# Order of the setup loads and of the second modulation in an adaLN block with windowed attention and a bilinear MLP

## The chip, the cores and the metric

The kernel runs on one core of one Trainium2 chip. The metric is the device time of one execution in microseconds (us). Three runs of the kernel before gave 594.92, 594.03 and 593.01 us, median 594.03. One further execution was recorded by the hardware profiler; its span, from the first to the last instruction, is 594.0 us, and every position below is given in us from the start of that span.

## The reference

The input `x` has 2048 rows of 576 numbers. One conditioning row `c` gives six vectors of 576, by `silu(c) @ w_mod`, with `w_mod` of 576 x 3456:

```
sa, ca, ga, sb, cb, gb = split(silu(c) @ w_mod, 6)
h = layernorm(x) * (1 + ca) + sa          # first modulation
x = x + ga * attention(h, wqkv, wo)       # each row looks at itself and 7 rows before, 2 apart; 32 heads of 18
h = layernorm(x) * (1 + cb) + sb          # second modulation
x = x + gb * ((h @ w_gate) * (h @ w_up)) @ w_down      # 4608 hidden columns
```

Matrices are bf16. Nearly all of the arithmetic is in the last line.

## The kernel before, in words

The rows are cut into ten chunks, four of 128 rows and six of 256 (`SIZES`, L34). Each chunk goes through `project` (LN, modulation, q, k and v; L424) and `attend` (logits, softmax, weighted sum, output projection `wo`, second LN and modulation into `h2T`; L499). Both are Python generators: each `yield` is a place where the caller can go on with something else, so the order in which the caller advances them is the order of the instructions. `gate_up` (L608) then runs the 4608 hidden columns for a pass of one or two chunks, in nine blocks of 512 columns, and `down` (L664) multiplies by `w_down`. While one pass of `gate_up` runs, a `Pacer` slips in the attention of the next chunk.

**The setup** is L737 to L777 and is the only part that the change touches. There the order on every computing engine is the order of the program (`manual_schedule` over all of them). It works off chunk 0 up to its `h2T` and chunk 1 up to its q, k and v, and in between makes the modulation vectors:

- `mod_columns` (L229) multiplies two of the six vectors' weights with the silu row by 40 small matmuls, so that they lie along partitions; `mod_pick` (L249) takes the right elements out by a multiplication with a diagonal and a sum on VectorE. It is called for `sa, ca` (buffer `wmA`) and for `sb, cb` (buffer `wmB`).
- `mod_row_mm` and `mod_row_copy` (L257, L264) make `ga` and `gb` as rows that are equal on all partitions, by ten matmuls each (L261) and two copies on ScalarE (L265, L266). Their weights are the two halves of `wmC`.
- `warm(n)` (L268) issues `n` matmuls on zeros, whose result nobody reads.

The three weight buffers come from a pool of two, so `wmB` takes the place of `wmA` once that has been used.

**Loads.** SyncE's queue (q1) brings `wqk`, `wv`, rows of `x` and the gate weights. GpSimd's queue (q0) brings, in the order of the program: both row loads of `load_first` (each made of a main part over 128 partitions and a rest over 64), `wo` in four loads of 32 partitions each (L200), the up weights of the hidden blocks (`load_up`, L205), the `gb` half of `wmC` (`load_gb`, L202), the stores of v to a DRAM scratch `vd` (L487), and the reloads of v shifted by the window into `vsh` (L497). A program order on GpSimd means that an issue which must wait holds back all later ones. Up weights of blocks 0 and 1 go to buffers of their own (`gm`), those of blocks 2 to 5 to places inside the buffer that `w_down` takes later (`wd`).

**Chunk 0's attention** has a form of its own: `attn` is shifted by eight small matmuls (`up`, L557), VectorE copies it (L558) and multiplies it with v (four L563), and 40 matmuls with shifted identities add the eight products up, transposed, into `oTs` (L573). Two copies (L587, L588), ten matmuls with `wo` (`pw`, L594), the gate by `ga` (L599), the residual (L600), then LN2 (L369 to L385), transposes (L406) and the second modulation (L416, L418) end in `h2T`.

The middle of the setup before:

```python
        go(b0, "up")        # chunk 0's logits and softmax
        next(a0, None)      # chunk 0's v
        next(a1)            # chunk 1's v
        load_up([1, 2, 3])
        mod_row_mm(wmC, 0)
        mod_row_copy(0, ga_bc)
        next(b0)            # up matmuls, first product
        pmB = mod_columns(wmB, 0)
        go(b0, "oT")
        mod_pick(pmB, 2)
        next(a1)            # chunk 1's first q
```

Of the kernel before, what the change touches and what calls it, by code (L numbers as in the profile page):

```python
# [18 lines left out]
D = 576  # L19
DP = 640  # L20
KT = 5
H = 32
DH = 18
# [36 lines left out]
def kernel(  # L60
# [13 lines left out]
    nc = tc.nc  # L74
# [40 lines left out]
    for sl, m0, off in ((slice(0, KT), 0, 0), (slice(KT, KT + 1), KT - 1, -64)):  # L115
        n = sl.stop - sl.start
# [9 lines left out]
    wo = wts.tile([P, KT, D], BF, name="wo")  # L126
# [23 lines left out]
    def load_rows(eng, dst, src):  # L150

        eng.dma_start(dst[:, 0:KT - 1, :], src[0:(KT - 1) * P, :].rearrange("(k p) n -> p k n", p=P))
        eng.dma_start(dst[0:64, KT - 1, :], src[(KT - 1) * P:D, :])
# [25 lines left out]
    def wm_tile():  # L179
        return sp.tile([P, KT, 2 * D], BF, name="wm", bufs=2)  # L180

    nc.sync.dma_start(c_row[:], c[0, :].rearrange("(m p) -> m p", p=64))
    wmA, wmC = wm_tile(), wm_tile()
# [8 lines left out]
    wmB = wm_tile()  # L192

    def load_first():

        load_rows(nc.gpsimd, wmC[:, :, 0:D], w_mod[:, 2 * D:3 * D])
        load_rows(nc.gpsimd, wmB, w_mod[:, 3 * D:5 * D])
        for dl in range(4):
            nk = len(range(dl, DH, 4))
            nc.gpsimd.dma_start(wo[dl * H:(dl + 1) * H, 0:nk, :], A_wo.rearrange("(h d) n -> h d n", d=DH)[:, dl::4, :])  # L200

    def load_gb():  # L202
        load_rows(nc.gpsimd, wmC[:, :, D:2 * D], w_mod[:, 5 * D:6 * D])

    def load_up(blocks):  # L205

        for b in blocks:
            load_gm(gu_blocks[b][0], b, 1, nc.gpsimd)

    def kp(kt):  # L210
        return slice(0, P) if kt < KT - 1 else slice(0, 64)

    def silu_c():

        pc = att([P, 10], BF, "pc")
        for o in range(2):
            nc.tensor.transpose(pc[64 * o:64 * (o + 1), 0:9], c_row[:], identw[0:9, HALO:HALO + 9])
        nc.vector.tensor_copy(c_f[0:64, :], pc[0:64, :].rearrange("p (k o) -> p k o", o=2)[:, :, 0])
        nc.vector.tensor_copy(c_f[64:, 0:KT - 1], pc[64:, 0:8].rearrange("p (k o) -> p k o", o=2)[:, :, 1])
        e_f = sp.tile([P, KT], F32, name="e_f")  # L220
        nc.scalar.activation(e_f[:], c_f[:], ACTF.Exp, scale=-1.0)
        nc.vector.tensor_scalar_add(e_f[:], e_f[:], 1.0)
        nc.vector.reciprocal(e_f[:], e_f[:])
        nc.vector.tensor_tensor(sc32[:], c_f[:, :, None].to_broadcast([P, KT, H]), e_f[:, :, None].to_broadcast([P, KT, H]), ALU.mult)
        nc.gpsimd.tensor_copy(sc_bc[:], sc32[:, :, 0:1].to_broadcast([P, KT, P]))

        nc.vector.tensor_reduce(diag[:], ident.rearrange("p (b j) -> p j b", j=32), axis=AX.X, op=ALU.add)

    def mod_columns(wm, fill):  # L229

        pm = ps_mlp.tile([P, 2, 512], F32, name="pm", tag="mlp")
        pv = pm[:, 0, 0:2 * KT * 32].rearrange("p (v m j) -> p v m j", v=2, j=32)
        for kt in range(KT):
            if fill and kt % 2 == 0:
                warm(fill)
            w = wm[kp(kt), kt, :].rearrange("p (v f) -> p v f", v=2)
            wmain = w[:, :, 0:512].rearrange("p v (m g j) -> p v m g j", g=4, j=32)  # L240
            for last in range(2):
                for g in range(4):
                    gs = slice(32 * g, 32 * g + 32)
                    rhs = w[:, :, 512 + 32 * (g % 2):544 + 32 * (g % 2)] if last else wmain[:, :, :, g, :]
                    nc.tensor.matmul(pv[gs, :, KT - 1, :] if last else pv[gs, :, 0:KT - 1, :], lhsT=sc32[kp(kt), kt, :], rhs=rhs,
                                     start=(kt == 0 and not last), stop=(kt == KT - 1), skip_group_check=True)
        return pv

    def mod_pick(pv, vi):  # L249
        pick = sp.tile([P, 2, KT, 32], F32, name="pick", bufs=1)  # L250
        nc.vector.tensor_tensor(pick[:], pv, diag[:, None, None, :].to_broadcast([P, 2, KT, 32]), ALU.mult)
        nc.vector.tensor_reduce(modc[:, vi:vi + 2, :], pick[:], axis=AX.X, op=ALU.add)
        nc.vector.tensor_scalar_add(modc[:, vi + 1, :], modc[:, vi + 1, :], 1.0)

# [2 lines left out]
    def mod_row_mm(wm, gi):  # L257
        pr = rows[gi] = ps_mlp.tile([P, 2, 512], F32, name="pr", tag="mlp")
        for b, c0, c1 in ((0, 0, 512), (1, 512, D)):
            for kt in range(KT):  # L260
                nc.tensor.matmul(pr[:, b, 0:c1 - c0], lhsT=sc_bc[kp(kt), kt, :], rhs=wm[kp(kt), kt, gi * D + c0:gi * D + c1],  # L261
                                 start=(kt == 0), stop=(kt == KT - 1))

    def mod_row_copy(gi, dst):  # L264
        nc.scalar.copy(dst[:, 0:512], rows[gi][:, 0, :])  # L265
        nc.scalar.copy(dst[:, 512:D], rows[gi][:, 1, 0:64])  # L266

    def warm(n):  # L268

        pw = ps_mlp.tile([P, 2, 512], F32, name="warm", tag="mlp")  # L270
        for _ in range(n):
            nc.tensor.matmul(pw[:, 0, :], lhsT=zeros[:, 0:P], rhs=zeros[:, 0:512], start=True, stop=True)
# [7 lines left out]
    def load_gm(gm, b, t, eng):  # L280
        eng.dma_start(gm[:, :, t, :], (B_w_gate, B_w_up)[t][0:(KT - 1) * P, b * FB * P:(b + 1) * FB * P].rearrange("(k p) n -> p k n", p=P))
# [73 lines left out]
    def setup_late():  # L355
        setup_guard.__exit__(None, None, None)
        late_once = pool("late", 1)
        late["hh"] = late_once.tile([P, FT, CM], BF, name="hh")
        late["gup"] = pool("gup", 2)
# [331 lines left out]
    def attend_into_place(ci):  # L691
        di, c0 = home[ci]
        if di not in h2T:
            h2T[di] = h2p.tile([P, KT, CM], BF, name="h2T")
        return attend(ci, h2T[di][:, :, c0:c0 + SIZES[ci]])
# [36 lines left out]
    def go(g, label):  # L732
        while next(g, None) != label:
            pass


    with tc.manual_schedule(engines=COMPUTE):  # L737
        a0, a1, b0 = project(0), project(1), attend_into_place(0)
        warm(5)
        silu_c()  # L740
        next(a0)
        warm(4)
        pmA = mod_columns(wmA, 1)
        mod_pick(pmA, 0)
        next(a0)
        warm(9)
        next(a0)
        load_first()
        load_up([0])
        load_gb()  # L750
        next(a1)
        go(a0, "qkr")
        next(a1)
        next(a0)
        go(a1, "v0")
        go(b0, "up")
        next(a0, None)
        next(a1)
        load_up([1, 2, 3])
        mod_row_mm(wmC, 0)  # L760
        mod_row_copy(0, ga_bc)
        next(b0)
        pmB = mod_columns(wmB, 0)
        go(b0, "oT")
        mod_pick(pmB, 2)
        next(a1)
        next(b0)
        go(b0, "ln2")
        go(a1, "qkr")
        next(b0)  # L770
        mod_row_mm(wmC, 1)
        warm(5)
        go(b0, None)
        go(a1, None)
        mod_row_copy(1, gb_bc)
        load_up([4, 5])
        setup_late()  # L777

    passes = [(di, p) for di, d in enumerate(DOWN) for p in d]
# [49 lines left out]
```

## Time and profile before

| what | value |
|---|---|
| device time, median of 3 (lowest to highest) | 594.03 us (593.01 to 594.92) |
| span of the profiled execution | 594.0 us |
| TensorE matmul busy | 574.0 us (97%), 5286 matmuls |
| VectorE, ScalarE, GpSimd busy | 316.3, 270.9, 61.6 us |
| bytes moved by DMA | 76.47 MB, of them q0 28.14 MB and q1 44.29 MB |
| first matmul of `gate_up` | at 43.21 us |
| mean granted TensorE clock | 0.994 of full speed |

The page gives shares over the whole span, and TensorE is busy nearly all of it. The setup is the first 43 us of that, and must be read by itself: from the answers that list the instructions in order of time, from the chain of waits cut to this stretch, and from the loads with their time from issue to landing. A row of the instruction list has the start, the busy time, the engine, the line and the tiles, and in brackets how long the engine stood idle before it and what ended that. A row of the windows has the stretch and its length, then busy us and count of instructions for PE, PE's weight loads, DVE, ACT and POOL, then the granted clock, the DMA engines' busy share and GB/s. A row of the DMA queues has packets, MB and the share of the 16 engines' time.

### The profile page before, as it was taken

How to read it: one execution, taken by the hardware profiler on the slowest of the kernel's cores; microseconds unless marked ns; L12 is line 12 of the kernel's file. 1: busy time of each engine (PE TensorE's matmuls, PEld its weight loads, DVE VectorE, ACT ScalarE, POOL GpSimd, SP SyncE). 2: the span in 40 equal slices, each digit the busy share in tenths (PEclk: the TensorE clock that was granted, in tenths of full speed). 3: DMA queues.
4: the chain of work that ended last, by engine and by line, in shares of the span. 5: the costliest groups of instructions: out<-in, count | busy, mean ns of one | idle time of the engine just before them, and what ended most of it. 6: DMA issues, size and time to landing. Idle time of an engine off the chain costs nothing.

```text
span 594.0 us, 12510 instructions
## 1 busy us (share of the span) xinstructions
PE 574.0 (97%) x5286; PEld 377.8 (64%) x5286; DVE 316.3 (53%) x706; ACT 270.9 (46%) x496; POOL 61.6 (10%) x116
## 2 busy tenths in 40 slices
PE   8599999999999999999999999999999999999997
PEld 4378888878977864554458874544447853444675
DVE  5658585766966864935467254934455421212101
ACT  3436757666553255556752144556540224545100
POOL 3341101020021121011000201011000000000000
PEclk9989999999999999999999999999999999999999
DMA  8999852547950053356200602357200005540000
GB/s 271 282 334 343 269 163 92 161 165 211 296 172 21 31 190 100 95 185 227 72 1 1 200 31 90 90 162 248 81 1 11 12 20 160 161 154 6 1 21 20
DMA packets 54058, 76.47 MB, mean 129 GB/s; under 512 B 3682, under 2 KB 46642, under 8 KB 54002
## 3 DMA queue, kind: packets, MB, share of 16 engines
q1 hardware_dynamic: 44066, 44.29, 24.8%
q0 software_dynamic: 7376, 28.14, 14.3%
q10 hardware_dynamic: 2560, 3.25, 1.7%
q8 instruction: 41, 0.67, 0.5%
q14 instruction: 15, 0.12, 0.1%
HBM read 70.93 MB, written 4.74 MB: 127 GB/s over the span
## 4 chain that ended last, share of the span: by engine, by line
PE 79%; DVE 7%; ACT 6%; DMA 6%; issue 2%; SPq 0%; ACTq 0%; POOL 0%; DVEq 0%
PE pgu L626 37%; PE acc L674 21%; PE pgu L635 6%; PE pq L455 5%; DMA wm<-in_w_mod_dram 3%; PE lgT L523 2%; ACT gu L643 2%; PE pvB L480 1%; DVE ln_stats L369 1%; PE pwA L594 1%; PE pwB L594 1%; PE pvA L480 1%; DMA vd<-v_sb 1%; DMA vd<-zeros 1%; ACT xn L387 1%
## 5 line engine op out<-in xcount | busy, mean ns | idle before, releaser
L626 PE MATMUL pgu<-h2T,gm 128*128 128x512 bf16 (+1 forms) x1504 | 239.7, 311 | 1.0 <-DVE h2T L416 0.7
L643 ACT CAST gu<-pgu 128x1024 bf16<-128x1024 f32 (+1 forms) x180 | 145.2, 842 | 105.4 <-PE pgu L635 77.7
L626 PEld LDWEIGHTS <-gm 128*128 128x128 bf16 x1504 | 118.5, 98 | 105.5 <-issue 14.9
L674 PE MATMUL acc<-wd,hh 128*128 128x288 bf16 x1152 | 147.2, 286 | 0.5 <-DVE y L680 0.5
L644 DVE TENSOR_TENSOR hh<-gu 128x512 bf16<-128x512 bf16 (+1 forms) x180 | 65.5, 368 | 135.6 <-ACT gu L643 134.9
L674 PEld LDWEIGHTS <-hh 128*128 128x128 bf16 x1152 | 112.1, 98 | 29.3 <-issue 1.2
L514 DVE TENSOR_TENSOR prod<-qT,kT 128x1280 bf16<-128x1280 bf16 (+1 forms) x80 | 46.7, 633 | 13.0 <-PE lgT L523 11.9
L680 DVE TENSOR_TENSOR y<-acc,gb_bc 128x576 bf16<-128x576 f32 (+1 forms) x17 | 12.3, 721 | 58.2 <-PE acc L674 58.2
L455 PE MATMUL pq<-hT,wqk 128*128 128x256 bf16 (+1 forms) x400 | 41.0, 251 | 0.0
L581 DVE TENSOR_TENSOR vsh<-vsh,attn 128x2304 bf16<-128x2304 bf16 x30 | 39.9, 1351 | 0.2
L497 POOL DMA_DIRECT2D vsh<-vd x30 | 22.4, 752 | 163.4 <-DVE hh L644 91.5
L387 ACT ACTIVATE xn<-x_t,ln_nmr,ln_rstd 128x576 bf16<-128x576 bf16 (+1 forms) x62 | 36.9, 645 | 1.7 <-issue 1.2
L635 PE MATMUL pgu<-h2T,gr 64*128 64x512 bf16 (+1 forms) x376 | 37.0, 311 | 0.0
L455 PEld LDWEIGHTS <-wqk 128*128 128x128 bf16 x400 | 32.3, 98 | 5.9 <-DVE ssum L547 1.3
L626 PE MATMUL pgu<-h2T,wd 128*128 128x128 bf16 x512 | 34.2, 219 | 0.3 <-ACT gu L643 0.3
L683 POOL DMA_DIRECT2D out_dram<-y x15 | 8.2, 549 | 250.6 <-DVE y L682 250.6
L626 PEld LDWEIGHTS <-wd 128*128 128x128 bf16 x512 | 30.4, 98 | 1.4 <-issue 0.6
L369 DVE BATCH_NORM_STATS2 ln_stats<-x_t 128x6 f32<-128x288 bf16 x64 | 26.4, 447 | 7.1 <-ACT ln_nmr L380 5.8
L635 PEld LDWEIGHTS <-gr 64*128 64x128 bf16 x376 | 12.2, 94 | 18.9 <-issue 11.5
L375 ACT ACTIVATE ln_rstd<-ln_rstd 128x2 f32<-128x2 f32 (+1 forms) x20 | 4.1, 203 | 38.2 <-DVE ln_rstd L372 38.2
L457 ACT CAST qT<-pq 128x512 bf16<-128x512 f32 (+1 forms) x20 | 10.1, 503 | 24.8 <-PE pq L455 24.8
L582 DVE TENSOR_TENSOR vsh<-vsh 128x2304 bf16<-128x2304 bf16 x15 | 20.2, 1349 | 0.0
(137 smaller groups left out, 476.9 us busy)
## 6 DMA issues: line engine op xcount, KB each, us to landing
vsh<-vd POOLq DMA_DIRECT2D x30, 576.0 KB, 6.0
gm<-in_B_w_gate_dram SPq DMA_DIRECT2D x29, 512.0 KB, 4.0
gm<-in_B_w_up_dram SPq DMA_DIRECT2D x27, 512.0 KB, 5.4
wd<-in_B_w_down_dram SPq DMA_DIRECT2D x4, 1152.0 KB, 6.2
out_dram<-y POOLq DMA_DIRECT2D x15, 144.0 KB, 2.0
wd<-in_B_w_gate_dram SPq DMA_DIRECT2D x4, 512.0 KB, 22.4
wd<-in_B_w_up_dram POOLq DMA_DIRECT2D x4, 512.0 KB, 10.5
gr<-in_B_w_gate_dram SPq DMA_DIRECT2D x29, 64.0 KB, 5.0
```

Source lines behind the costliest of these rows:

```text
L369: nc.vector.bn_stats(stats[:, j, hf, :], src[j][:, hf * 288:(hf + 1) * 288])
L387: nc.scalar.activation(xn[:, j0 + j, d0], src[j][:, s0:], ACTF.Identity, bias=nmr[:, j:j + 1], scale=rstd[:, j:j + 1])
L455: nc.tensor.matmul(pq[:, gi, 0:C], lhsT=wqk[:, kt, w0:w0 + P], rhs=h[:, kt, :], start=(kt == 0), stop=(kt == KT - 1))
L497: nc.gpsimd.dma_start(vsh[:].rearrange("p w d h -> p w (d h)"), src)
L514: nc.vector.tensor_tensor(prod[:, 0:nm, 0:C], qT[:, 0:nm, 0:C], kT[:, 0:nm, off:off + C], ALU.mult)
L581: nc.vector.tensor_tensor(vsh[:], vsh[:], attn[:, j, ws, None, :].to_broadcast([P, WG, DH, H]), ALU.mult)
L582: nc.vector.tensor_tensor(va[:], va[:], vb[:], ALU.add)
L626: nc.tensor.matmul(out[:, t, n, 0:C], lhsT=gu_blocks[b][0][:, kt, t, (i + n) * P:(i + n + 1) * P], rhs=h2[:, kt, cs], start=(first and n = ...
L635: nc.tensor.matmul(out[:, t, n, 0:C], lhsT=gu_blocks[b][1][rows, (i + n) * P:(i + n + 1) * P], rhs=h2[rows, KT - 1, cs], start=(first and ...
L643: nc.scalar.copy(g, ps[u][:, :, :, 0:C].rearrange("p t n c -> p n t c"))
L644: nc.vector.tensor_tensor(hh[:, fs, cs], g[:, :, 0, :], g[:, :, 1, :], ALU.mult)
L674: nc.tensor.matmul(acc[:, q, 0:288], lhsT=hh[:, f, j * P:(j + 1) * P], rhs=wd[:, f, q * 288:(q + 1) * 288], start=(f == 0), stop=(f == FT ...
```

## The change

`load_first` now brings `wmB` ahead of the `ga` half of `wmC`, and `wo` in five loads, of which four go over all 128 partitions and the last over 64; the resulting contents of `wo` are the same. `load_gb` moves ahead of the first `load_up`. `mod_pick` is cut in two, so that the multiplication can be issued early and the sum late. In the setup, `mod_columns(wmB)` and the multiplication come directly after chunk 0's v, ahead of the `up` matmuls; the `ga` row comes after them; chunk 1's v and its first q move from ahead of chunk 0's weighted sum to behind its output projection; the numbers of warm matmuls change from 4 to 7, and from 5 (behind the `gb` row) to 3 (ahead of chunk 0's `oT`); and the up weights of block 3 go from the second group of loads to the last one.

```diff
     def load_first():
+        load_rows(nc.gpsimd, wmB, w_mod[:, 3 * D:5 * D])
         load_rows(nc.gpsimd, wmC[:, :, 0:D], w_mod[:, 2 * D:3 * D])
-        load_rows(nc.gpsimd, wmB, w_mod[:, 3 * D:5 * D])
-        for dl in range(4):
-            nk = len(range(dl, DH, 4))
-            nc.gpsimd.dma_start(wo[dl * H:(dl + 1) * H, 0:nk, :], A_wo.rearrange("(h d) n -> h d n", d=DH)[:, dl::4, :])
+        for k in range(KT):
+            nd = min(4, DH - 4 * k)
+            nc.gpsimd.dma_start(wo[0:nd * H, k, :], bass.AP(A_wo.tensor, A_wo.offset + 4 * k * D, [[D, nd], [DH * D, H], [1, D]]))
...
-    def mod_pick(pv, vi):
+    def mod_pick(pv):
         pick = sp.tile([P, 2, KT, 32], F32, name="pick", bufs=1)
         nc.vector.tensor_tensor(pick[:], pv, diag[:, None, None, :].to_broadcast([P, 2, KT, 32]), ALU.mult)
+        return pick
+
+    def mod_sum(pick, vi):
         nc.vector.tensor_reduce(modc[:, vi:vi + 2, :], pick[:], axis=AX.X, op=ALU.add)
...
-        warm(4)
-        pmA = mod_columns(wmA, 1)
-        mod_pick(pmA, 0)
+        warm(7)
+        mod_sum(mod_pick(mod_columns(wmA, 1)), 0)
...
         load_first()
+        load_gb()
         load_up([0])
-        load_gb()
...
         next(a0, None)
-        next(a1)
-        load_up([1, 2, 3])
+        pmB = mod_columns(wmB, 0)
+        pick = mod_pick(pmB)
+        load_up([1, 2])
+        next(b0)
         mod_row_mm(wmC, 0)
         mod_row_copy(0, ga_bc)
-        next(b0)
-        pmB = mod_columns(wmB, 0)
         go(b0, "oT")
-        mod_pick(pmB, 2)
-        next(a1)
+        mod_sum(pick, 2)
+        warm(3)
         next(b0)
         go(b0, "ln2")
         go(a1, "qkr")
         next(b0)
         mod_row_mm(wmC, 1)
-        warm(5)
         go(b0, None)
         go(a1, None)
         mod_row_copy(1, gb_bc)
-        load_up([4, 5])
+        load_up([3, 4, 5])
```

## The prediction

> **What bounds the kernel now.** The page has TensorE busy for 97% of the span, and from the first `gate_up` matmul at 43.21 us to the end its waits are short. Where the setup ends, everything behind it starts; so I read the setup by itself, first with the chain of waits cut to it.
>
> ```profile
> 15.04 14.42 DMA wm<-in_w_mod_dram
> 29.46 0.14 issue
> 29.60 1.64 PE pm L245 x36
> 31.24 0.43 PE oTsA L573 x3
> ...
> 36.16 1.42 PE pw L594 x10
> ...
> 40.32 0.21 ACT ln_rstd L375
> ...
> 43.73 1.37 PE pgu L626 x22
> ```
>
> Columns are start, length and what. The load of `wmB` lasts until 29.46; in-order TensorE meets `pm` ahead of the 40 `oTs` matmuls, which have had their products since 28.5. Next, the stretches (clock, DMA share and GB/s stand last):
>
> ```profile
> 20.00:24.00 4.00, 3.75 (x32) 2.47 (x27) 2.22 (x5) 2.02 (x6) 0.79 (x2) 1.00 1.03 315
> 24.00:30.00 6.00, 1.56 (x27) 1.02 (x30) 3.19 (x5) 0.76 (x3) 0.98 (x2) 0.83 1.08 215
> 30.00:34.00 4.00, 4.00 (x62) 3.12 (x51) 1.15 (x3) 0.00 (x0) 2.72 (x5) 0.50 1.04 287
> ```
>
> TensorE idles from 25.15 to 29.6 (1.56 us busy of six), its clock falls to half at 28.0 and returns at 34.8. The DMA engines are busy all along, yet move only 215 GB/s in that stretch, where 315 to 350 is usual around it. Then the loads by landing, and GpSimd's queue:
>
> ```profile
> wm<-in_w_mod_dram POOLq DMA_DIRECT2D x1, 1152.0 KB, 14.4
> wo<-in_A_wo_dram POOLq DMA_DIRECT2D x2, 180.0 KB, 15.1
> ```
> ```profile
> 23.21 0.77 POOL L281 DMA_DIRECT2D gm<-in_B_w_up_dram  x1 [4.54 <-DMA wm<-in_w_mod_dram]
> ...
> 39.79 1.49 POOL L497 DMA_DIRECT2D vsh<-vd  x2 [4.71 <-DMA vd<-v_sb]
> 41.27 1.49 POOL L281 DMA_DIRECT2D wd<-in_B_w_up_dram  x2
> ```
>
> GpSimd's ninth load waits for its first to land, and the eleventh and thirteenth likewise wait for the third and fifth: eight are in flight at most. The reloads `vsh` wait for v's store.
>
> **What the Trainium skill says.** "DMA: Bandwidth & Descriptors", section on queues, rings and completion order: each DMA engine takes packets from its queues in turn. The trace agrees: from 18 to 20 us q0 moved 152 packets and q1 124, but 0.58 against 0.11 MB, since q0's are larger; so while q0 has work, it sets its own pace. "SBUF — State Buffer", section "Door 1": a transfer's rate hangs on how many of 16 ports its partitions reach; partitions 0 to 63 reach only eight. The trace fits: q0's bytes up to 24.0 us (1.72 MB) are the `ga` row and nearly all of `wmB`, so the slow stretch is `wo` (32 partitions a load) with their tails. It does not prove it, since q1 carried a load over 64 partitions then. "TensorE: Matmul & The Clock Gate", Part 1: half clock after an idle window of about 3.4 us, full again after a busy one. The trace agrees with the falls and returns above.
>
> **The change, part by part.** I sum against the profiled span, 594.0, which is the median of the three runs (594.03).
>
> *wmB first.* Its first bytes still move at about 17.5 (the issue at 13.62 follows the `wqr` copy, as before). By 18.0 q0 has moved 0.11 MB, then 0.27 MB per us. wmB's main part, 1.18 MB, is thus through for the mean engine at 18 + 1.07/0.27 = 22.0. Landings trail that mean: the `ga` row by 3.2 us (19.7 against 22.9), the second `vsh` load by 1.0 (48.2 against 49.2). I take 2.8, nearer to the case at this place: wmB lands at 24.8 (23.0 to 25.2 by these bounds).
>
> *ga row second, wo over all partitions.* Its main part ends at 1.92 MB: mean 24.7, landing 27.5 (25.7 to 27.9), if the rate holds, which is what the new `wo` is to do. If it does not, the same bytes landed at 30.1 before.
>
> *TensorE's order.* v of chunk 0 ends at about 22.0 (20.71 plus half of 2.61). `pm` 24.8 + 1.64 = 26.4; `up` 0.36, 26.8. On VectorE the multiplication (0.49) lies ahead of the `attn_up` copy (0.42): ready 27.4; four products, 2.76: 30.15. TensorE meanwhile does the `ga` row, 27.5 + 1.70 = 29.2, then 40 `oTs` matmuls at full clock, 40 x 0.055 = 2.2: 31.4. The last products are in time. From the end of `oTs` to the end of `pw` it took 2.05 before (35.53 to 37.58), so `pw` ends at 33.45. *Clock:* idle is 22.0 to 24.8, 2.8 us, less than a window, but before, a window with 0.56 us of work counted as idle. Cost between 0 and 2.7 (all 40 at 0.104 each, 4.2 us, and the row at an estimated 2.4, from 0.427 for a cold 512-column warm matmul). I take 0.7, as a stay at full clock is somewhat likelier: `pw` ends at 34.15, against 37.58, **3.4 gained**.
>
> *Chunk 1's v and q behind `pw`.* Not free: ScalarE's order now puts v's two copies and all q and k copies ahead of LN2's Ln. v takes 10 x 0.122, q and k 4 x 0.62 on TensorE, the last copy 0.37: 4.1 us after `pw`. Before, Ln ran at 40.32, 2.74 after it. **1.4 lost** (1.0 to 2.0: PSUM buffers may add waits). The five warm matmuls that leave (1.25 us) and the `gb` row (1.70, until 5.4 after `pw`) lie in TensorE's wait for LN2's result (5.5 after it): nothing. The early multiplication lies in TensorE's `up`, the late sum (0.66) beside `oTs`: nothing. `warm(3)` runs in the 0.56 us of the oT copy and may delay `pw` by 0.1 to 0.3, within the clock's margin. `warm(7)` adds 3 x 0.43 to a queue that waited 0.84 for `wmA`; of the 0.3 to 0.4 left, all is hidden, as q waits for `wqk`, whose landing at 12.6 set the `wqr` copy.
>
> So `gate_up` starts 3.4 - 1.4 = **2.0 earlier**, at 41.2.
>
> *GpSimd's queue.* v of chunk 1 is stored some 1.95 after `pw`, at 36.1 instead of 31.86. The `gb` row, block 0's and 1's up weights wait for landings from 25 to 29 us, and are wanted at 38 and later, with 10 us to spare. The `vsh` reloads wait for the store: 5.6 later (its row at 61.66; the two bounds are 2.0, the quiet ones, and 7.4): 41.7 against 39.79. Block 3's up weights are now behind them, where block 4's were, and those landed 12.1 after the first `vsh` issue: 53.8. TensorE wants them at about 53.1 before, hence 51.1 now. That is a wait of 2.7 at worst. But q0 is empty from about 36 to the reloads, 5 us in which q1 moves some 300 packets per us instead of 75, and so is largely done when they come; then two `vsh` and block 3 need 1.70 MB at up to 0.35 per us. Bounds 0 to 2.7; behind a wait there, VectorE's and ScalarE's work also catches up. I take **0.8 lost**. `vsh` itself lands by some 50, and VectorE wants it at 50.9 (52.87 before).
>
> Passes 0 to 3 are ordered by a planner, whose order may change with the setup: 0.7 either way, an estimate (their idle gaps are about 0.7 in each 10 us).
>
> Sum: 594.0 - 3.4 + 1.4 + 0.8 = **592.8 us**.
>
> **The rivals.** *The full gain:* the clock stays up (0.7) and the up weights come in time (0.8): 591.3; with landings at the early bounds (wmB 23.0, VectorE's last product then 28.35, `pw` at 31.6) 589.5 to 590. For it: the idle time is shorter than a window, and q1 will be ahead. Against it: the store of v is 4 us later, and everything up to block 3 hangs on it.
>
> *Slower, by the ga row:* it was off the path at 22.9, and now stands in front of all 40 `oTs` matmuls. If the slow stretch comes from the 64-partition load on q1 or from slow engines rather than from `wo`, the row lands at 30.1; at half clock it ends at 32.5 and `oTs`, partly at half clock, 3.4 later at 35.9; `pw` ends at 37.95, `gate_up` starts at 37.95 + 5.63 + 1.4 = 45.0, 1.8 later; with the 0.8 that is 596.6. It decides from a landing at about 28.7 on, where the sum is zero. For it: the trail of 3.2 us, and that the order within these 1.99 MB does not change their sum. Against it: 215 GB/s fits the ports of `wo`.
>
> *Given back in pass 0:* the whole 2.7 is paid, 594.7; also possible in part.
>
> **How the numbers follow.** Forecast 0.55 (591.4 to 594.0 alone), full gain 0.17, ga row 0.18, given back 0.10. About 0.3%, 1.8 us, is what a measurement can tell from no change. Faster by more: 0.17 and 0.25 of the forecast's share, 0.42. Slower by more: the ga row's 0.18 and some of what is given back, 0.04, together 0.22. Within: 0.36. The range reaches from 590.0 to 596.6.
>
> **What would show it.** `pm` begins near 24.8 (right to 25.5); the `ga` row's load lands before 28.7; GB/s from 24 to 30 near 300; PEclk 1.00 or a short half; `pw` ends near 34; Ln about 4.1 behind it; first `gate_up` near 41.2; and a wait of the first block-3 matmul for a DMA of under 1 us. A dip that stays with the new `wo`, or Ln not waiting for the k copies, would make the working wrong.

## The result, and the profile after

The changed kernel is slower: median 602.23 us of four runs (601.27 to 603.69) against 593.95 (593.01 to 594.92), ratio 1.0141, 95% interval 1.0115 to 1.0168. The forecast was 592.8, range 590.0 to 596.6. The profiled span grew from 594.0 to 600.0.

I begin with the chain of waits of the changed kernel, cut to the setup and pass 0 (start, length, what; lines below L253 have moved down by three).

```profile
14.42 13.06 DMA wm<-in_w_mod_dram
27.48 0.14 issue
...
36.83 1.24 PE pv L483 x10
38.07 0.02 issue
38.09 0.70 ACT v_sb L487 x2
38.79 0.29 ACT qT L460
39.08 0.01 issue
39.08 7.02 DMA vd<-v_sb
46.10 0.28 issue
46.39 1.50 POOL vsh L500 x2
47.88 10.34 DMA wd<-in_B_w_up_dram
58.22 0.05 issue
58.27 0.61 PE pgu L629 x4
```

In the kernel before, the same view ran from `pw` through LN2 into `gate_up`. Now it runs from `pw`'s end, 36.83, into chunk 1's v, its store on GpSimd's queue at 39.08, the 7.02 us until that has landed, the `vsh` reloads, and block 3's up weights behind them, which land at 58.2. LN2 isn't on it any more. What TensorE did meanwhile stands in the list of instructions by time, first of the kernel before, then of the changed one:

```profile
49.50 0.61 PE L626 MATMUL pgu<-h2T,wd 128*128 128x128 bf16 x8
...
52.58 1.06 PE L626 MATMUL pgu<-h2T,wd 128*128 128x128 bf16 x16
53.47 0.72 PE L455 MATMUL pq<-hT,wqk 128*128 128x128 bf16 x10
```
```profile
49.57 0.61 PE L629 MATMUL pgu<-h2T,wd 128*128 128x128 bf16 x8
...
52.65 0.83 PE L629 MATMUL pgu<-h2T,wd 128*128 128x128 bf16 x12
58.27 0.61 PE L629 MATMUL pgu<-h2T,wd 128*128 128x128 bf16 x4 [4.79 <-DMA wd<-in_B_w_up_dram]
```

Up to 53.4 the two are level to 0.07 us: the first use of `wd`, block 2, is at 49.50 and 49.57. Then the changed kernel stands still for 4.79. The stretches of the changed kernel (columns as before: busy us of PE, weight loads, DVE, ACT, POOL, then clock, DMA share, GB/s) show what comes with it:

```profile
24.00:30.00 6.00, 4.13 (x54) 1.86 (x54) 4.05 (x8) 0.00 (x0) 3.26 (x5) 0.50 1.14 214
30.00:34.00 4.00, 4.00 (x36) 3.34 (x35) 0.10 (x1) 0.70 (x2) 1.67 (x4) 0.50 1.11 255
54.00:58.00 4.00, 0.00 (x0) 0.00 (x0) 3.08 (x4) 0.00 (x0) 0.00 (x0) 1.00 1.04 348
58.00:61.00 3.00, 2.73 (x26) 2.73 (x27) 2.32 (x3) 0.37 (x1) 0.00 (x0) 0.51 1.05 347
```

After the pause the clock is at 0.51 for 3 us, so about 1.4 us of full-speed work is lost. "TensorE: Matmul & The Clock Gate", Part 1, in the Trainium skill says that an idle window is followed by half clock until a busy one has passed; 4.79 us of idleness and 3 us of half clock agree. 4.8 and 1.4 make 6.2, and the first `vsh` multiplication of the next attention starts 6.2 later too (87.98 against 81.82). The spans differ by 6.0: nothing else of size is lost behind it. The first two rows show the other surprise: from 24 to 30 us the loads still move 214 GB/s, where the new form of `wo` was to lift them to about 300.

**From spans to times.** The device times differ by 8.3, the spans by 6.0. A profiled execution's device time is about 2.1 above its span (602.13 and 600.0 for the changed kernel). The one of the kernel before took 596.1, which is 2.1 above the median of its runs. It was thus a slow one: of 98 other executions of the kernel before, which took 592.45 to 596.79 (spans of 590.3 to 594.7), only two were slower. Most of the 2.3 by which the two differences differ is that; a profile of a typical execution isn't on record, so where one stands at 53.4 us isn't known.

### The profile page after: what moved, and what is told of

Same layout as the page of the kernel before. It is cut to its first block, busy times and chain, and to the rows that moved or that the text cites. A ratio compares the mean times of both kernels' runs of the same rounds, so it can differ in the third digit from the quotient of the medians.

```text
span 600.0 us, 12476 instructions
## 1 busy us (share of the span) xinstructions
PE 575.6 (96%) x5252; PEld 380.3 (63%) x5287; DVE 316.2 (53%) x706; ACT 271.1 (45%) x496; POOL 62.5 (10%) x117
## 3 DMA queue, kind: packets, MB, share of 16 engines
q0 software_dynamic: 7872, 28.15, 14.4%
## 4 chain that ended last, share of the span: by engine, by line
PE 80%; DMA 7%; ACT 5%; DVE 5%; issue 2%; POOL 0%; SPq 0%; ACTq 0%
PE pgu L629 37%; PE acc L677 21%; PE pgu L638 5%; PE pq L458 5%; DMA wm<-in_w_mod_dram 3%; PE lgT L526 2%; DMA wd<-in_B_w_up_dram 2%; DMA vd<-v_sb 2%; ACT gu L646 2%; PE pvB L483 1%; PE pvA L483 1%; PE pwA L597 1%; PE pwB L597 1%; ACT xn L390 1%; PE turnA L409 1%
## 5 line engine op out<-in xcount | busy, mean ns | idle before, releaser
L629 PE MATMUL pgu<-h2T,gm 128*128 128x512 bf16 (+1 forms) x1473 | 237.0, 310 | 2.8 <-issue 1.0
L517 DVE TENSOR_TENSOR prod<-qT,kT 128x1280 bf16<-128x1280 bf16 (+1 forms) x80 | 46.9, 633 | 12.9 <-PE lgT L526 11.8
L683 DVE TENSOR_TENSOR y<-acc,gb_bc 128x576 bf16<-128x576 f32 (+1 forms) x17 | 12.2, 720 | 58.2 <-PE acc L677 58.2
L483 PEld LDWEIGHTS <-hT 128*128 128x128 bf16 x160 | 15.7, 101 | 6.9 <-issue 2.3
```

The costliest lines, as they stand in the source:

```text
L483: nc.tensor.matmul(pv[q][:, 0:288], lhsT=h[:, kt, j * P:(j + 1) * P], rhs=wv[:, kt, q * 288:(q + 1) * 288], start=(kt == 0), stop=(kt == K ...
L517: nc.vector.tensor_tensor(prod[:, 0:nm, 0:C], qT[:, 0:nm, 0:C], kT[:, 0:nm, off:off + C], ALU.mult)
L629: nc.tensor.matmul(out[:, t, n, 0:C], lhsT=gu_blocks[b][0][:, kt, t, (i + n) * P:(i + n + 1) * P], rhs=h2[:, kt, cs], start=(first and n = ...
```

## The experiments

**Theory L** (the queue): chunk 1's v is stored late, the `vsh` reloads wait for the store, and block 3's up weights, now behind them, come after TensorE wants them. **Theory K** (the clock): half clock from 17.1 to 34.2 us sets the loss. **Theory R** (reloads): VectorE's wait for `vsh` (1.9 us in two waits) sets it, and block 3 is a bystander.

### One half of L undone at a time

`a1_block3_back` is the changed kernel with block 3's up weights in the first group:

```diff
-        load_up([1, 2])
+        load_up([1, 2, 3])
...
-        load_up([3, 4, 5])
+        load_up([4, 5])
```

> The changed kernel with one part undone: block 3's up weights are loaded in the second group again, ahead of chunk 1's v store and the vsh reloads. Theory L (the loss is up weights that land late, because they stand behind the reloads, which wait for a store that is now late): TensorE's 4.8 us wait at block 3 goes; block 4's up weights are now first behind the reloads and land near 58.5, where TensorE wants them at about 57.5, so a wait of about 1 us is left, and VectorE's 1.9 us for vsh stays: about 598 (596.5 to 599.5). Theory K (the loss is the half clock from 17.3 to 34.2 in the setup): no change, 602. Theory R (the loss is the late vsh reload, which holds VectorE and with it the whole of chunk 1's attention; block 3's wait only lies beside it): at most 1 us gained, 601 to 602.

`a2_v_early` is the changed kernel with chunk 1's v directly behind chunk 0's:

```diff
         next(a0, None)
+        next(a1)
         pmB = mod_columns(wmB, 0)
```

> The changed kernel with one part undone: chunk 1's v is multiplied directly behind chunk 0's v again, so that its store leaves early; block 3's up weights stay in the last group. Theory L: store issued near 30, landed by 39.5, reloads issued near 40, block 3's up weights landed near 52 where TensorE wants them at 53: the 4.8 us and the 1.9 us go, and the 1.3 us of v leaves the stretch behind pw: 594 to 596. Theory R: the same. Theory K: the clock in the setup is as in the changed kernel, so 601 to 602.

`a3_both_back` has both.

> The changed kernel with both parts undone, block 3's load and chunk 1's v. Theory L: no wait for up weights at all; 593.5 to 596, within 0.5 us of the kernel with v alone put back. Theory K: 601 to 602. If this is faster than the kernel with v alone put back by over 1 us, v's early store did not free the queue by itself.

Measured: 599.59 (ratio to the kernel before 1.0093 [1.0074, 1.0111]), 596.78 (1.0050 [1.0035, 1.0065]) and 595.63 (1.0033 [1.0021, 1.0045]). Of the 8.3, a1 takes back 2.6, a2 5.4, both 6.6. GpSimd's queue in a2, from the instruction list (start, length, what, and in brackets the idle time before it and its end):

```profile
34.16 0.55 POOL L490 DMA_DIRECT2D vd<-v_sb  x1 [2.43 <-DMA wo<-in_A_wo_dram]
...
41.20 1.49 POOL L500 DMA_DIRECT2D vsh<-vd  x2 [3.65 <-DMA vd<-v_sb]
42.69 2.23 POOL L284 DMA_DIRECT2D wd<-in_B_w_up_dram  x3
```

The store is issued 4.9 earlier than in the changed kernel, everything behind it 5.2 earlier, and no matmul of pass 0 waits for a load. `gate_up` started at 43.15, no sooner than the changed kernel's 42.73, and yet the kernel is 5.4 faster: K falls, and so does the reading that these 5.4 us lie ahead of `gate_up`. In a1 block 3 is no longer waited for, but `vsh` is still late. The groups of a1 from 36 to 90 us that waited for a load (busy us and mean ns, then idle us and what ended it):

```profile
L629 PE MATMUL pgu<-h2T,wd 128*128 128x128 bf16 x167 | 12.0, 219 | 1.0 <-DMA wd<-in_B_w_up_dram 1.0
...
L584 DVE TENSOR_TENSOR vsh<-vsh,attn 128x2304 bf16<-128x2304 bf16 x4 | 5.3, 1355 | 2.1 <-DMA vsh<-vd 2.1
```

R would have left a1 at the full loss, since VectorE's wait is still there, at 2.1; it lost 2.6 of it. So R falls as the sole cause. It isn't nothing, though. a1 is 4.0 slower than a3, from which it differs only by the late v. TensorE has two waits in a1's profile that a3's lacks: 1.0 for block 4's up weights, and 1.1 more for a copy of k,

```profile
63.34 0.41 PE L483 MATMUL pvB<-wv,hT 128*128 128x288 bf16 x2 [1.65 <-ACT kT L468]
```

against 0.55 in a3. ScalarE, which makes that copy, had waited 1.9 for VectorE, and VectorE for `vsh`. So the late store costs by two ways: up weights, and `vsh`.

L's ranges were a little low: a1 is 0.1 above its range and a2 0.8. And a3 is 1.2 faster than a2, where L allowed 0.5; a2's profile shows no wait for a load in pass 0, so that this rest has no explanation yet.

### The same two edits on the kernel before

`b1_block3_late_in_before` moves block 3's loads alone:

```diff
-        load_up([1, 2, 3])
+        load_up([1, 2])
...
-        load_up([4, 5])
+        load_up([3, 4, 5])
```

> The kernel before with one part of the change alone: block 3's up weights go behind the reloads, v stays early. Theory L: reloads issued near 39 to 40, block 3's up weights landed near 52 (as block 4's were) against a want at 53.1; blocks 4 and 5 land 1.9 and 3.8 us later, wanted at 57 and 61: no wait, 593.5 to 594.5; the two parts hurt only together. Theories K and R: 594 as well. A rise of over 2 us would say that the place of the load alone is enough.

`b5_both_in_before` also takes both `next(a1)` out of the middle, so that v and the first q of chunk 1 come with `go(a1, "qkr")` behind `pw`.

> The kernel before with the two suspected parts together and nothing else of the change: chunk 1's v and first q behind chunk 0's output projection, and block 3's up weights in the last group of loads. Theory L: each alone is harmless or small (block 3 alone measured 594.07), together v's store leaves near 38.5, the reloads near 45 to 46, block 3's up weights land near 57 to 58 against a want near 53: a wait of 4 to 5 us on TensorE, 599 to 601. If it stays under 596, the order of the row loads and of TensorE's work in the changed kernel is needed for the loss, and theory L is incomplete.

b1: 594.07, ratio 1.0005 [0.9998, 1.0012], 20 runs. b5: 597.72, ratio 1.0056 [1.0031, 1.0080]. Moving block 3 alone costs nothing that can be measured; together with the late v it costs 3.3, less than the 5 to 7 expected (its store left at 36.5 and not at 38.5). GpSimd's queue in b1 and then in b5, and the group that waits in b5:

```profile
28.83 0.54 POOL L487 DMA_DIRECT2D vd<-v_sb  x1 [0.64 <-DMA wo<-in_A_wo_dram]
...
36.86 1.49 POOL L497 DMA_DIRECT2D vsh<-vd  x2 [5.49 <-DMA vd<-v_sb]
38.34 2.23 POOL L281 DMA_DIRECT2D wd<-in_B_w_up_dram  x3
```
```profile
36.54 0.55 POOL L487 DMA_DIRECT2D vd<-v_sb  x1 [4.02 <-ACT qT L457]
...
42.34 1.50 POOL L497 DMA_DIRECT2D vsh<-vd  x2 [5.26 <-DMA vd<-v_sb]
43.84 2.23 POOL L281 DMA_DIRECT2D wd<-in_B_w_up_dram  x3
```
```profile
L626 PE MATMUL pgu<-h2T,wd 128*128 128x128 bf16 x176 | 13.5, 230 | 3.1 <-DMA wd<-in_B_w_up_dram 3.1
```

Block 3's issue at 38.3 is in time, at 43.8 it costs a wait of 3.1, and at 47.9, in the changed kernel, of 4.8. So L's chain is shown from both sides, and the size goes with the store. But the two edits don't weigh the same. In the changed kernel the late v alone (a1 against a3) costs 4.0, the late block 3 alone (a2 against a3) 1.2, both together 6.6. The late v alone was not run on the kernel before, so it isn't shown that both edits are needed there.

b1 also shows what an earlier start is worth: its `gate_up` began at 39.19, 4.0 ahead of the profile before, its span is only 1.6 shorter, and 1.7 us were lost on a wait for the gate rests `gr` on q1.

### The loads

`b2_wo_five_in_before` puts only the new `wo` loads into the kernel before; `a7_both_back_old_wo` is a3 with the old ones; `b3_load_order_in_before` puts only `wmB` ahead of the `ga` row and `load_gb()` ahead of `load_up([0])`.

> The kernel before with the five wo loads alone. Theory P (the step of the prediction: 32 partitions a load reach half of the ports, and 128 lift the rate): over 290 GB/s from 24 to 30, wmB and wo land earlier, 0 to 2 us faster. Theory S (each row of 1152 bytes is a packet of its own in the new form, as the changed kernel's 219 packets for 0.24 MB on q0 between 24 and 26 us suggest, and packets are taken in turn with q1's, so q0 moves less): packets of q0 between 24 and 32 near 1.1 KB, the last wo load lands 2 us later or more, v's stores and the reloads behind it too; 594 to 596.

> The kernel with v and block 3 put back, with wo in four loads of 32 partitions again. Theory S: the ga row and wo land 1 to 2 us earlier than with five loads, gate_up starts near 42.5 instead of 43.9: 593.5 to 595, that is 1 to 2 us faster than 595.63. Theory P: slower than 595.63, by 0 to 2. If it stays at 595.6, the rest of the loss lies in the order of the rows and of TensorE's work alone.

> The kernel before with the order of the row loads alone: wmB first, then the ga row, wo in its old four loads, the gb row ahead of block 0's up weights. TensorE still meets the ga row ahead of the up matmuls, so it waits for the ga row near 27 to 28 with wmB long there, and the products on VectorE start only then. If the rest of 1.2 us between the kernel with all but the orders put back (595.03) and the kernel before comes from the order of the rows, this gives 594.5 to 597; if from TensorE's order, 593.5 to 594.5.

b2: 595.54, ratio 1.0026 [1.0016, 1.0036]: the five loads cost 1.5 in the kernel before. a7: 595.03, 1.0024 [1.0013, 1.0034], which can't be told from a3's 1.0033. What a7 still has over the kernel before, 1.2 us, must lie in the other edits. b3: 596.63, 1.0039 [1.0027, 1.0051]; there TensorE keeps the old order and waits 5.3 us for the `ga` row, so it shows that an order of loads has to go with TensorE's order, not what the new order costs by itself. The stretches of b2:

```profile
24.00:30.00 6.00, 3.43 (x63) 2.41 (x63) 3.80 (x7) 0.70 (x2) 1.43 (x3) 0.72 1.14 189
30.00:34.00 4.00, 4.00 (x40) 3.38 (x38) 0.72 (x3) 0.00 (x0) 1.77 (x3) 0.57 1.15 204
```

`wo` over 128 partitions moves no more than over 32 (215 and 287 in the profile before). So the prediction's reading of the stretch, the ports that 32 partitions reach, is wrong for it. Theory S had the right sign but the wrong packets: in the traces the five loads add 496 packets of 16 bytes to q0 (7872 packets in all instead of 7376), while the data still goes in packets of 4608 bytes. The 1.1 KB was a mean of the two. From 24 to 26 us the changed kernel's q0 had 219 packets with 0.24 MB beside 224 of q1, the kernel before 112 with 0.37 MB beside 110. So the queues did go in turn, and a packet of 16 bytes used up a turn like a large one.

Three further forms of the kernel seek another reason for the slow stretch. `d1_rest_later` issues the loads over 64 partitions on q1 (L302) behind the gate weights:

```diff
+        return slots
+
+    def load_kept_rest(slots):
...
-            load_kept()
+            slots = load_kept()
...
+    load_kept_rest(slots)
```

> The kernel before, with the two loads of 64 partitions on SyncE's queue (the last 64 rows of the kept blocks) behind the gate weights instead of ahead of them. If these loads make the slow stretch (about 215 GB/s between 24 and 30 us, in this kernel and in the changed one), that stretch is gone there, over 290 GB/s, and comes where they now move. If wo makes it, 24 to 30 stays below 240. The time may rise by up to 5 us, since block 2's last matmuls want these rows at 51.

`d2_wo_in_row_order` fetches `wo`'s rows in the order in which they lie in memory, so that the output projection is computed with permuted weights:

```diff
-        for dl in range(4):
-            nk = len(range(dl, DH, 4))
-            nc.gpsimd.dma_start(wo[dl * H:(dl + 1) * H, 0:nk, :], A_wo.rearrange("(h d) n -> h d n", d=DH)[:, dl::4, :])
+        for k0 in (0, 2):
+            nc.gpsimd.dma_start(wo[:, k0:k0 + 2, :], A_wo[k0 * P:(k0 + 2) * P, :].rearrange("(k p) n -> p k n", p=P))
+        nc.gpsimd.dma_start(wo[0:64, KT - 1, :], A_wo[(KT - 1) * P:D, :])
```

> The kernel before, with wo loaded in the order of its rows (two loads of 128 partitions and one of 64, two rows of 1152 bytes a partition) instead of regrouped by head, so the output projection is computed with permuted weights. Bytes are the same. If the form of the wo loads makes the slow stretch, it is gone: over 290 GB/s between 24 and 30, wmB landed before 27. If the loads of 64 partitions on SyncE's queue make it, it stays below 240.

`e1_wo_contiguous` keeps the order from head to head, but gives each partition four neighbouring rows, 4608 bytes in one piece (the columns of v are reordered to match); `e2_changed_order_contiguous` is a3 with the same.

> The kernel before with another order of v's columns, so that each partition's four rows of wo are one stretch of 4608 bytes in memory: one load over 128 partitions and one over 64 instead of four over 32; each copy of v out of PSUM becomes two. If the slow stretch comes from rows that are fetched apart, 24 to 30 moves near 300 GB/s, wmB lands before 27, as with wo in row order, and the time is 591 to 592.5. If it comes from the 20.7 KB between the heads' rows in memory, the stretch stays below 250 and the time within 593 to 595; ScalarE's 30 added copies of about 0.2 us may cost up to 1.

> The changed kernel with v and block 3 put back and the same contiguous wo loads. If wo's packets were what spoiled the changed order, wmB lands near 24, the ga row near 26.5 and wo by 28, gate_up starts before 40: 590.5 to 592, under the kernel before with contiguous wo. If the changed order brings nothing by itself, it is equal to that kernel or up to 1.5 slower.

d1, one execution: 608.75, with a 13.8 us wait for the rests; from 24 to 30 us 251 GB/s. That lies between the two marks set for it, and where those loads were left in place, the profiles have 215 (the kernel before) to 249 (a7), so d1 by itself settles nothing. d2, one execution: 591.43, span 589.4. e1: 602.35, ratio 1.0139 [1.0117, 1.0161]; e2: 602.73, 1.0140 [1.0118, 1.0162]. The stretches of d2, then of e1:

```profile
24.00:30.00 6.00, 4.39 (x75) 3.36 (x74) 4.31 (x8) 0.70 (x2) 2.70 (x5) 0.72 1.06 312
30.00:34.00 4.00, 4.00 (x56) 3.33 (x54) 1.20 (x3) 0.81 (x3) 0.68 (x1) 1.00 1.03 339
```
```profile
24.00:30.00 6.00, 2.94 (x60) 2.13 (x60) 3.64 (x6) 0.70 (x2) 1.09 (x2) 0.73 1.14 191
30.00:34.00 4.00, 4.00 (x39) 3.38 (x37) 0.69 (x3) 0.00 (x0) 0.00 (x0) 0.55 1.06 202
34.00:38.00 4.00, 0.64 (x12) 0.47 (x9) 0.56 (x1) 0.65 (x2) 0.00 (x0) 0.88 1.05 217
```

The stretch is slow in every form that jumps from head to head (18 rows, 20,736 bytes), on 32 partitions or 128 and in pieces of 1152 or 4608 bytes, and it is gone when the rows are read in order, with the loads over 64 partitions still in place. The packets in the traces say the same: from 24 to 30 us a 4608-byte packet of q0 took 339 ns on average in the kernel before, 344 in b2 and 330 in e1, but 240 in d2, and q1's 1024-byte packets beside them took 90, 103, 95 and 62. So the other queue is slowed too. Why jumps of this length are slow, no run shows.

e1's and e2's loss of 8 us was in none of their expectations. In e1 TensorE waits 5.7 us for `wo`, which lands only at 40.24, 12 us after the rest of `wmB`. Meanwhile q0 moved 1.77 MB, more than twice the bytes of `wo`. Why `wo` was overtaken by what was issued behind it stays open, so e1 tests longer pieces by its rate and its packets, not by its time.

### Row order with the right columns

d2 is 1.0 us faster than the fastest of the 98 executions, and so suggests a kernel that beats both: `wo` in row order, and the columns of o written in the order (h d), so that they meet those rows. `f1_row_order_in_before` is the kernel before with d2's loads and

```diff
-                nc.vector.tensor_tensor(vsh[:, w0 % WG:w0 % WG + 2],
+                nc.vector.tensor_tensor(vsh[:, w0 % WG:w0 % WG + 2].rearrange("p w d h -> p w (d h)").rearrange("p w (h d) -> p w d h", d=DH),
...
-                nc.vector.tensor_tensor(o_sb[:, j, 0:D].rearrange("p (d h) -> p d h", d=DH), va[:, 0], va[:, 1], ALU.add)
+                nc.vector.tensor_tensor(o_sb[:, j, 0:D].rearrange("p (h d) -> p d h", d=DH), va[:, 0], va[:, 1], ALU.add)
```

`f2_row_order_in_changed_order` is a3 with the same.

> The kernel before, with wo kept in row order: three loads of consecutive rows (1152 bytes each) in place of four that skip from head to head, and the columns of o written in the order (h d) by the two VectorE lines that make them (the products of chunk 0, the last sum of the later chunks), so that the output is the reference's. Theory M (the slow stretch comes from the order in which wo's rows are fetched): 24 to 30 us moves 290 to 320 GB/s as in d2_wo_in_row_order, wo is there early, gate_up starts at 38 to 40 us, and the median falls by 1 to 3 us, to 591 to 593, as most of an earlier start has been given back in every run so far. Rival (the permuted writes cost VectorE what the loads give): the products of chunk 0 and the last sum become over 20% longer, and the median is 594 or more.

> The changed order with block 3's loads and the v store put back (a3_both_back), with wo in row order and o's columns in the order (h d), as in f1_row_order_in_before. Theory M: 24 to 30 us moves about 300 GB/s against 214 in the changed kernel, and the median falls by 2 to 4 us against a3_both_back's 595.6, to 591.5 to 593.5. If the order of the row loads costs 1.2 us by itself, as a7 against the kernel before says, it ends about 1 us above f1_row_order_in_before; if the two are equal, that 1.2 us was itself a delay behind wo.

f1: 620.54, ratio 1.0443 [1.0428, 1.0458]; f2: 622.29, 1.0482 [1.0468, 1.0497]. The loads do what they should, 298 and 295 GB/s from 24 to 30 us, but the rival wins by far. VectorE's groups of f1:

```profile
L584 DVE TENSOR_TENSOR o_sb<-vsh 128x576 bf16<-128x576 bf16 x15 | 39.5, 2631 | 0.3
...
L563 DVE TENSOR_TENSOR vsh<-v,attn_up 128x1152 bf16<-128x1152 bf16 x4 | 19.9, 5241 | 0.1
```

The same groups took 454 and 754 ns in the kernel before. Written in steps of 36 bytes, the last sum is 5.8 times as long and a product 7.0 times. The four products lie in the setup: 19.9 us instead of 2.8, and `gate_up` starts at 57.65. So this is no version that beats the kernel before, and none was found: d2's gain of 2.5 us, seen in a single execution, would need a reordering that costs less. Whether the new order of row loads costs 1.2 us by itself, f1 against f2 can't say, since both wait for VectorE.

## Why the prediction was wrong

**The step that failed** is GpSimd's queue: "Bounds 0 to 2.7 ... I take 0.8 lost". It is 4.8 of wait and 1.4 of half clock behind it. The mechanism was named, with its place, and as a rival ("given back in pass 0"); its price was too low even at its upper bound. That the forecast was out by more than this one term comes from the others below. By its terms:

- The v store's issue was put at 36.1 and came at 39.08. `pw` ended 2.7 later than forecast, 2.0 of it since half clock held throughout (below), the rest mostly since the `ga` row then took 2.9 instead of the 2.4 allowed for; 0.3 is v's and q's copies.
- The store's landing was taken as 5.6, from a later store. The same store in the kernel before was issued at 31.86 and landed 7.4 later; here it took 7.02. The nearest row was the right one, and was kept only as a bound. The reason is GpSimd's own queue, on which the transfers of the setup landed in the order of their issue in both profiles: block 2's up weights, issued at 33.17, landed at 43.02, the rows of `x` behind them at 43.58 and 44.02, and the store at 46.10. "DMA: Bandwidth & Descriptors", section on the anatomy of one DMA, gives a fixed cost of about 2 us, mostly until the last write is confirmed. The 15 stores of results agree (2.1 us). This store landed 2.1 after the transfer ahead of it.
- From the reloads to block 3's landing: 12.1 forecast, 11.8 measured.
- TensorE wanted the load at 53.48, not at 51.1. It was still 4.8 early.

The wait of 2.7 was discounted to 0.8 because "q0 is empty from about 36 to the reloads" and q1 would be "largely done". Neither was so. q0 had the up weights of blocks 1 and 2 and the rows of `x` to bring until 44, and as it emptied, SyncE went on to later blocks' loads, which it issued from 41.77 on instead of from 50.63. The DMA queues of the changed kernel from 40 to 42 us, then from 46 to 48 (packets, MB, share of 16 engines' time):

```profile
q0 software_dynamic: 151, 0.50, 73.9%
q1 hardware_dynamic: 172, 0.18, 29.0%
```
```profile
q1 hardware_dynamic: 702, 0.70, 109.8%
```

A queue that lies idle is not bandwidth saved up for its next load: here the other queue took all of it for work of its own, and still had some when the reloads came.

**Where the sum stood.** "594.0, which is the median of the three runs" set a span equal to device times. The profiled execution took 596.1, so the sum began 2.1 above the typical execution, and in spans the forecast was 592.8 against 600.0. Those 7.2 are 1.5 from a later `gate_up` than forecast, 4.0 from the wait above the 0.8, 1.4 from the clock after it, and some 0.5 of the earlier start that was gone by block 2, less 0.2 of rounding. In a typical execution there may have been less to gain: b1, whose setup differs from the kernel before only in block 3's load, started `gate_up` at 39.19 in its profiled execution, ahead of the forecast 41.2. No profile shows where the kernel before starts it typically.

**The other steps.** *wmB first*: right, `pm` began at 24.1 (24.8). *The ga row*: landed at 27.48 (27.5), so the slower rival, which decides from 28.7, did not come; but the number was right by luck. The rate wasn't lifted, it stayed at 214 GB/s, and q0 had a head start that the working didn't have: its first load was issued at 12.99 instead of 13.62, and by 18.0 us it had moved 0.38 MB, where 0.11 were assumed. *wo*: the reading by ports was wrong (b2), and the price of the 496 small packets was missed, though packets that are taken in turn were part of the prediction. *Clock*: 0.7 of a possible 2.7 was taken; in the profiled execution the whole 2.7 was paid, half clock from 17.1 to 34.2. It isn't what made the loss: three more executions had a mean clock of 0.989 instead of 0.983, some 7 us less of half clock, and spans of 599.1 to 601.5. *LN2*: Ln came 3.9 after `pw` (4.1, right), but `gate_up` started 5.9 after it where the sum had 7.03. The kernel before had VectorE on chunk 2's LN statistics ahead of the modulation there, which the sum carried over. *Chunk 1's v behind `pw`*: what it costs LN2 was worked out; that it also leads the only queue that feeds block 3 was worked out and then discounted.

Of the 8.3 us, then, 6.6 go away when v and block 3 are put back: that is L, with its second way over `vsh`. The remaining 1.7 lie in the other edits. The new `wo` loads cost 1.5 in the kernel before and 0.6, within the intervals, in the changed order. The rest, the order of the row loads, of TensorE's work and of the warm matmuls, was not taken apart.

## What to carry to other kernels

When a step is moved, follow the queue that its result is stored on to the last load behind it, and set every link at what the same transfer took at the same load; don't credit idle time of one DMA queue to the next load of that queue while another queue has work to issue. A move that is free by itself (block 3's loads in the kernel before: ratio 1.0005) can be expensive beside another (3.3 us with the late v), when the other sets the time from which its load counts. And before summing, compare the profiled execution's own device time with the other runs, not its span.

## What the hardware showed that was not expected

- A VectorE operation on bf16 whose output is written in steps of 36 bytes took 5.8 and 7.0 times as long (2631 instead of 454 ns for 576 elements, 5241 instead of 754 for 1152). "SBUF — State Buffer", section "Door 1", says that accesses which cross to a new 16-byte line pay a penalty; the direction agrees, the size is this case's own.
- Loads of 1152-byte rows that lie 20,736 bytes apart held the DMA engines to 189 to 251 GB/s in the stretch from 24 to 30 us, on 32 partitions and on 128; the same bytes in row order moved at 295 to 312.
- The five `wo` loads brought 496 packets of 16 bytes with them, and each took a turn of its queue: q0 moved 0.24 MB from 24 to 26 us instead of 0.37.
- A store of 144 KB needed 7.0 to 7.4 us to land behind earlier transfers of its own queue, against 2.1 for the stores of results.
- An earlier start can be mostly given back: b1's 4.0 us at `gate_up` left 1.6 at the end, since 1.7 went into a wait for a load of the other queue.
